# Twenty loads of the value cache, each issued as two transfers of 120 and 8 partitions

## The chip, the core and the metric

The kernel runs on one core of a Trainium2 chip. The core has five engines: TensorE (PE in the profile, with its weight loads as PEld), VectorE (DVE), ScalarE (ACT), GpSimd (POOL) and SyncE (SP). Data come from HBM (the tensors' home) into SBUF, a memory of 128 partitions, by DMA: 16 DMA engines work side by side, and a transfer is issued by an instruction of SP or ACT and tells of its landing on a semaphore. The metric is the device time of one execution in microseconds; the median of the runs is given.

## What is computed

A decode step of two alternating layer kinds, each applied twice to a residual stream x of 4 tokens (one per batch entry, width 448): attention over a cache, then a feed-forward layer. Only the last 2048 positions of the 8192 in the cache are used.

```python
def _A_ref(x, k_cache, v_cache, wq, wo):
    B, Sq, D = x.shape
    Hq, Dh = 16, 256
    Hkv, Sk = k_cache.shape[1], k_cache.shape[2]          # 8, 8192
    W = min(4096, max(256, Sk // 4))                      # 2048
    rep = Hq // Hkv
    q = (x @ wq).reshape(B, Sq, Hq, Dh).transpose(0, 2, 1, 3)
    k = jnp.repeat(k_cache[:, :, Sk - W:, :], rep, axis=1)
    v = jnp.repeat(v_cache[:, :, Sk - W:, :], rep, axis=1)
    p = _softmax(jnp.einsum("bhqd,bhkd->bhqk", q, k) * (Dh ** -0.5), axis=-1)
    o = jnp.einsum("bhqk,bhkd->bhqd", p, v)
    return o.transpose(0, 2, 1, 3).reshape(B, Sq, Hq * Dh) @ wo

def _B_ref(x, w_gate, w_up, w_down):
    return (_silu(x @ w_gate) * (x @ w_up)) @ w_down

x = x + _A_ref(_layernorm(x), A_k_cache, A_v_cache, A_wq, A_wo)
x = x + _B_ref(_layernorm(x), B_w_gate, B_w_up, B_w_down)
# ... and both once more, with the same caches and weights
```

All tensors are bf16. Both attention passes use the same keys and values.

## The kernel before, in words

**Units of work.** An attention pass over one token t (0 to 3) in layer l (0 or 1) and one key-value head kvh (0 to 7) is a *unit*, written as three digits "tlk". For a unit the kernel needs the keys (2048 x 256, 1 MB, two cells of SBUF) and the values (1 MB, loaded as two halves hv = 0 and 1 of 512 KB, one cell each). A cell is 4 KB in each of the 128 partitions; there are 31 cells and 7 more that are free once the q weights have been used for the last time. A value half is 1024 positions, eight of them in each partition: row q of a half is 4 KB that lie together in HBM, and goes to partition q.

**What happens to a unit.** DVE transposes the keys in place (`tr`, L887). PE forms the scores (`scores`, L920), the softmax goes over DVE, ACT and PE in small steps (L936 to L992), PE multiplies by the values (`pv`, L1001; its operand is the cell of the value half), then the result is turned (L1025), scaled (L1035) and sent through the output projection (L1047, L1055). When a token's eight heads are through, its residual, its norm, its feed-forward layer (L666 to L783) and the next q projection follow.

**Held data.** `HOLD` lists the keys and values that stay in their cells from layer 0 to layer 1. The others are loaded again for layer 1. In all SP issues 158 DMAs: 83 value halves (L897), 56 loads of keys (L875 for whole 1 MB ones, L881 for halves), 18 loads of x and weights (L521), one store.

**Order.** Nothing is planned at run time. `PLAN` gives the units' groups, `SEQ_PE`, `SEQ_DVE`, `SEQ_ACT`, `SEQ_POOL` and `SEQ_SP` the order of the instructions of each engine, by hand or by a search made before; `SLOTS` gives the cell of each load in SP's order. `Graph` finds which instruction must wait for which and places the waits (`_place_waits`). A load waits on SP until the last reader of its cell is through, and all loads behind it on SP wait with it. Each cell (or first cell of a pair) has a semaphore `h<cell>` of its own; a load adds 16 to it when it has landed (`_count`, `emit`), and its readers wait for the sum so far.

**Filler.** Entries `w1`, `w3` ... in `SEQ_PE` are matmuls of zeros into the accumulator A (L1137, and L543 when one follows another). They change no value.

**Places that matter here.** `Op` and `_count` (the amount that a load adds), `emit` (which issues it and attaches the semaphore), and in `group` the loop over `hv`, which makes one load per value half:

```python
g.dma(1 << 19, lambda e, cell=cell, hv=hv, vsrc=vsrc: e.dma_start(unit(cell), vsrc[hv]), None,
      w=(f"v{t}_{kvh}_{hv}",), cells=(cell,))
```

Of the kernel before, what the change touches and what calls it, by code (L numbers as in the profile page):

```python
# [34 lines left out]

ROWF = (1, 2)
PLAN = (
# [122 lines left out]

class Op:
    __slots__ = ("i", "eng", "kind", "emit", "deps", "nbytes", "dsem", "dval", "start", "end", "pos", "waits", "inc",
                 "val", "known", "cells", "rel", "bank", "tag", "run")

    def __init__(self, i, eng, kind, emit):
        self.i, self.eng, self.kind, self.emit = i, eng, kind, emit
        self.deps = {}
        self.nbytes = 0  # L170
        self.dsem = None
        self.dval = 0
        self.cells = self.rel = self.bank = ()
        self.inc = False
        self.val = 0
        self.waits = []


class Graph:
    tag = last_a = before = None  # L180
# [50 lines left out]

    def _count(self, o, sem):
        o.dsem = sem
        self.dcount[sem] = self.dcount.get(sem, 0) + 16
        o.dval = self.dcount[sem]

    def schedule(self, filler):
# [82 lines left out]
    def emit(self, eng_name, eng, sems, dsems):  # L320
        for o in self.order[eng_name]:
            for d in o.waits:
                if d.dsem is not None:
                    eng.wait_ge(dsems[d.dsem], d.dval)
                else:
                    eng.wait_ge(sems[d.eng], d.val)
            ins = o.emit(eng)
            if eng_name == PE:
                self.before = o.kind
            if o.dsem is not None:  # L330
                ins.then_inc(dsems[o.dsem], 16)
            elif o.inc:
                ins.then_inc(sems[eng_name], 1)
# [11 lines left out]
def build(nc, A_x, A_k_cache, A_v_cache, A_wq, A_wo, B_x, B_w_gate, B_w_up, B_w_down, out):  # L345
    s0 = A_k_cache.shape[2] - WIN
    g = Graph()

    with ExitStack() as es:
# [105 lines left out]
        for a in range(4):  # L455
            g.op(DVE, "d1", lambda e, a=a: e.memset(qmask[32 * a:32 * a + 32, a:a + 1], DH ** -0.5), r=("qmask",),
                 w=(f"qmask{a}",))
# [31 lines left out]
        for s_ in range(NS):  # L489
# [9 lines left out]
             w=("hmask",))  # L499
# [6 lines left out]
        for P in range(2):  # L506
# [5 lines left out]
             w=("lomask",))  # L512
# [334 lines left out]
        def unit(cell):  # L847
            return kv[:, HALF * cell[0]:HALF * cell[0] + HALF]

        def which(cell, kc):  # L850
            return int(cell[0] == max(kc[0][0], kc[1][0]))
# [7 lines left out]
        def group(gi, members, outs, split):  # L859
# [7 lines left out]
            for pp, t, layer, kvh in members:  # L867
                if layer == 1 and (t, kvh) in k_held:
                    kc, kk = k_held.pop((t, kvh))
                else:  # L870
                    kc, kk = [[], []], [f"k{pp}_{hf}" for hf in range(2)]
                    ksrc = A_k_cache[t, kvh, s0:s0 + WIN, :].rearrange("(p j) d -> p (j d)", p=128)
                    g.tag = ("k", t, layer, kvh)
                    if f"{t}{layer}{kvh}" in WHOLE.split():
                        g.dma(1 << 20, lambda e, kc=kc, ksrc=ksrc: e.dma_start(  # L875
                            kv[:, HALF * kc[0][0]:HALF * kc[0][0] + 2 * HALF], ksrc[:, :]), None, w=tuple(kk), cells=tuple(kc),
                            run=8192)
                    for hf, cell in enumerate(kc):
                        if f"{t}{layer}{kvh}" not in WHOLE.split():
                            g.tag = ("k", t, layer, kvh)  # L880
                            g.dma(1 << 19, lambda e, cell=cell, kc=kc, ksrc=ksrc: e.dma_start(  # L881
                                unit(cell), ksrc[:, HALF * which(cell, kc):HALF * which(cell, kc) + HALF]), None, w=(kk[hf],),
                                cells=(cell,))

                        def tr(e, cell=cell):
                            a = unit(cell).bitcast(UINT32).rearrange("p (k s) -> p k s", k=32)
                            return e.transpose(a, a)  # L887
                        g.tag = ("t", t, layer, kvh)
                        g.op(DVE, "tr", tr, w=(kk[hf],))
                vsrc = A_v_cache[t, kvh, s0:s0 + WIN, :].rearrange("(a q g) d -> a q (g d)", a=2, q=128)  # L890
                vs = [[], []]
                for hv, cell in enumerate(vs):
                    g.tag = ("v", t, layer, kvh, hv)
                    if layer == 1 and (t, kvh, hv) in v_held:
                        vs[hv] = v_held.pop((t, kvh, hv))
                    else:
                        g.dma(1 << 19, lambda e, cell=cell, hv=hv, vsrc=vsrc: e.dma_start(unit(cell), vsrc[hv]), None,  # L897
                              w=(f"v{t}_{kvh}_{hv}",), cells=(cell,))
                keep_k = layer == 0 and f"k{t}{kvh}" in HOLD.split()
                keep_v = [layer == 0 and f"v{t}{kvh}{hv}" in HOLD.split() for hv in range(2)]  # L900
                kcs.append(kc)
                kks.append(kk)
                vss.append(vs)
                free_k.append(not keep_k)
                free_v.append([not x for x in keep_v])
                if keep_k:
                    k_held[(t, kvh)] = (kc, kk)
                for hv in range(2):
                    if keep_v[hv]:
                        v_held[(t, kvh, hv)] = vs[hv]  # L910
# [3 lines left out]
            def scores(e, Ps):  # L914
                last = None
                for ce in range(8):
                    for x in range(X):
                        for P in Ps:
                            qd = 64 * P + 32 * x
                            last = e.matmul(Sb[s_][qd:qd + 8, 0:32 * 2 * J],  # L920
                                            lhsT=qe[q_][:, P, ce, :, :].rearrange("p a n -> p (a n)"),
                                            rhs=keys(kcs[P], J * x, J, ce), start=(ce == 0), stop=(ce == 7),
                                            skip_group_check=True)
                return last
# [5 lines left out]
            parts = [(P,) for P in range(n)] if split else [tuple(range(n))]  # L930
            for Ps in parts:
                kw = dict(acc=(f"s{s_}",)) if Ps[0] else dict(w=(f"s{s_}",))
                o = g.op(PE, "sch" if split else f"sc{n}" + "w" * (two - n + 1), lambda e, Ps=Ps: scores(e, Ps),
                         r=tuple(k for P in Ps for k in kks[P]) + tuple(f"qe{q_}_{P}" for P in Ps), bank=(f"S{s_}",), **kw)
# [61 lines left out]
            def pv(e, P, hv):  # L996
                last = None
                M = 4 if n == 1 else 8
                for a in range(2):
                    for gg in range(4):  # L1000
                        last = e.matmul(Yb[p_][32 * gg:32 * gg + M, 256:512],  # L1001
                                        lhsT=pT[pt][:, gg, 2 * a + hv, 4 * P:4 * P + M] if n == 2 else
                                        pf[:, 16 * gg + 8 * a + 4 * hv:16 * gg + 8 * a + 4 * hv + 4] if two else
                                        p1[:, gg % 2, 2 * a + gg // 2, hv, :, :].rearrange("p y n -> p (y n)"),
                                        rhs=unit(vss[P][hv])[:, 1024 * a + 256 * gg:1024 * a + 256 * gg + 256], start=False,
                                        stop=False, skip_group_check=True)
                return last
            for P, (pp, t, layer, kvh) in enumerate(members):
                for hv in range(2):
                    kw = dict(acc=(f"y{p_}",)) if hv or P else dict(w=(f"y{p_}",))  # L1010
                    o = g.op(PE, "pv", lambda e, P=P, hv=hv: pv(e, P, hv), r=(f"pT{pt}", f"v{t}_{kvh}_{hv}"),
                             bank=(f"Y{p_}",), **kw)
# [5 lines left out]
                 w=("oh",), bank=(f"Y{p_}",))  # L1018
# [49 lines left out]
        for si, (heads, splits) in enumerate(zip(plan(), plan_splits())):  # L1068
            where = {}
            for batch, split in zip(heads, splits):  # L1070
                members, outs = [], []
                for m in batch:
                    pos += 1
                    t, layer, kvh = m
                    done[(t, layer)] = done.get((t, layer), 0) + 1
                    if kvh not in where:
                        ts = sorted(t_ for b in heads for t_, _, k_ in b if k_ == kvh)
                        where[kvh] = (oc % 2, ts)
                        if used[oc % 2] != ts:
# [3 lines left out]
                                 w=tuple(f"oT{oc % 2}_{t_}" for t_ in range(B)))  # L1083
# [25 lines left out]
            for t, layer in full:  # L1109
                residual(t)  # L1110
                norm(t, xr)
                if layer == 0:
                    with_, waiting = waiting, []
                    if t in ROWF:
                        ffn_row(with_ + [t])
# [25 lines left out]
        dsems = {d: es.enter_context(nc.semaphore(f"d_{d}")) for d in g.dcount}  # L1141
# [60 lines left out]
```

## Time and profile before

| | |
|---|---|
| time, median of 3 runs | 277.35 us (276.79 to 277.89) |
| span of the profiled execution, first to last instruction | 277.7 us |
| HBM read | 100.77 MB, 363 GB/s over the span |
| DMA queue of the loads (q1) | 100.78 MB, 91.8% of 16 engines |
| instruction fetches (q8, q14) | 36 of 16 KB and 9 of 8 KB, 0.9% and 0.1% of 16 engines |
| PE, DVE, POOL, ACT busy | 242.4, 185.0, 80.4, 62.8 us |
| granted TensorE clock, mean | 0.984 |

No time of the profiled execution is given but its span; it lies within the three runs' times, and so stands for them.

How to read the rows. In a row of a window stand its bounds and length, then for PE, PEld, DVE, ACT and POOL the busy time with the number of instructions, then the granted clock, the mean busy share of the 16 DMA engines, and GB/s. A DMA share a little over 1 comes from packets whose records overlap by some nanoseconds. In a row of the chain in order of time stand start, length and what was worked on; "DMA half<-in_A_v_cache_dram" with a length is the time from the issue of a load to its landing, the time that it waited behind earlier loads included. A queue's row has packets, MB and the time of its packets as a share of 16 engines. In a row of issues the last number is the median time from issue to landing. In a row of a tile's instructions, a/b/c is the shortest, median and longest duration in ns.

### The profile page before, as it was taken

The page shows a single profiled execution, that of the slowest core. Times are in us where ns is not written, and L with a number is a line of the kernel's source. Part 1 is how long each engine was busy: PE and PEld are TensorE (multiplying, and loading weights), DVE is VectorE, ACT ScalarE, POOL GpSimd, SP SyncE. Part 2 cuts the span into 40 slices and gives each one's busy share as a digit, 9 for nine tenths or more (in the row PEclk, how much of TensorE's full clock was granted, in tenths as well). Part 3 has the DMA queues.
Part 4 walks back from the last instruction along what each step waited for, and adds up shares of the span by engine and source line. Part 5 has one row for each costly group of instructions (what it writes and reads, how often), then busy time and mean ns, then how long its engine had stood idle before and what let it go on. Part 6 is the DMA issues. An engine that isn't in the chain of part 4 may idle for free.

```text
span 277.7 us, 10576 instructions
## 1 busy us (share of the span) xinstructions
PE 242.4 (87%) x4751; PEld 126.5 (46%) x4576; DVE 185.0 (67%) x574; ACT 62.8 (23%) x173; POOL 80.4 (29%) x224
## 2 busy tenths in 40 slices
PE   3997999999999887998888887979799787989995
PEld 0121232233475553544445444535455456667664
DVE  4666817735612687978857599986768757389841
ACT  0003021111112222331332333224132321232411
POOL 1160121111024221615044243133234332254350
PEclk9998899999999999999999999999989999999998
DMA  7999999999999999999999999999999998799200
GB/s 278 425 420 413 415 395 418 399 401 406 405 387 417 411 412 414 410 409 411 351 394 400 414 417 411 408 413 408 358 384 350 411 378 297 279 396 411 81 2 3
DMA packets 25740, 101.44 MB, mean 365 GB/s; under 512 B 2523, under 2 KB 6623, under 8 KB 21471
## 3 DMA queue, kind: packets, MB, share of 16 engines
q1 hardware_dynamic: 25687, 100.78, 91.8%
q8 instruction: 36, 0.59, 0.9%
q14 instruction: 9, 0.07, 0.1%
q10 hardware_dynamic: 8, 0.00, 0.0%
HBM read 100.77 MB, written 0.00 MB: 363 GB/s over the span
## 4 chain that ended last, share of the span: by engine, by line
PE 40%; DMA 36%; DVE 14%; issue 3%; ACT 2%; SPq 2%; POOL 2%; DVEq 0%; ACTq 0%
DMA half<-in_A_v_cache_dram 24%; DMA half<-in_A_k_cache_dram 12%; DVE half L887 8%; PE S L920 8%; PE A L543 6%; PE Y L1001 6%; PE A L1137 5%; PE Z L740 3%; PE A L1055 2%; PE Z L776 2%; PE A L1047 1%; PE Y L969 1%; SPq L521 1%; DVE oh L1019 1%; SPq L897 1%
## 5 line engine op out<-in xcount | busy, mean ns | idle before, releaser
L887 DVE STREAM_TRANSPOSE half<-half 128x1024 uint32<-128x1024 uint32 x86 | 104.7, 1229 | 8.8 <-DMA half<-in_A_k_cache_dram 8.8
L1137 PE MATMUL A<-identb,small 128*128 128x512 bf16 x139 | 53.3, 389 | 3.3 <-DVE A L447 2.9
L1015 POOL TENSOR_TENSOR small<-small 128x2 f32<-128x2 f32 (+1 forms) x48 | 38.5, 805 | 47.1 <-DVE small L992 29.7
L543 PE MATMUL A<-identb,small 128*128 128x512 bf16 x175 | 51.8, 397 | 0.0
L920 PE MATMUL S<-half,qe 128*8 128x128 bf16 (+1 forms) x1520 | 45.0, 240 | 6.6 <-issue 2.8
L1001 PE MATMUL Y<-half,pT 128*8 128x256 bf16 (+1 forms) x1024 | 42.9, 274 | 8.4 <-DMA half<-in_A_v_cache_dram 5.0
L920 PEld LDWEIGHTS S<-half,qe 128*8 128x8 bf16 x1520 | 30.5, 84 | 22.3 <-DVE half L887 9.8
L954 ACT ACTIVATE praw<-S,small 104x128 bf16<-104x128 f32 (+2 forms) x48 | 19.4, 404 | 68.3 <-DVE small L950 64.1
L1019 DVE SCALAR_TENSOR_TENSOR oh<-oh,small,Y 128x256 bf16<-128x256 bf16 x48 | 22.5, 468 | 16.9 <-ACT oh L1017 16.7
L926 POOL TENSOR_TENSOR qe<-qc,tiny 128x64 bf16<-128x64 bf16 x64 | 18.1, 294 | 43.9 <-PE S L920 35.2
L1001 PEld LDWEIGHTS Y<-half,pT 128*8 128x8 bf16 (+1 forms) x1024 | 20.2, 84 | 23.0 <-DVE small L992 6.5
L1017 ACT ACTIVATE oh<-Y 128x256 bf16<-128x256 f32 x48 | 18.4, 383 | 45.8 <-PE Y L1001 37.3
L1137 PEld LDWEIGHTS A<-identb,small 128*128 128x128 bf16 x139 | 14.6, 105 | 14.9 <-issue 8.9
L577 POOL TENSOR_SCALAR st<-st 128x1 f32<-128x1 f32 x16 | 4.3, 267 | 57.6 <-DVE st L567 56.4
L978 ACT ACTIVATE pT<-Y 128x64 bf16<-128x64 f32 (+1 forms) x48 | 12.4, 258 | 36.0 <-PE Y L969 29.6
L1055 PE MATMUL A<-wo_sb,oT 128*4 128x448 bf16 x192 | 17.5, 356 | 2.0 <-issue 1.1
L1082 POOL MEMSET oT<- 128x16 bf16 x39 | 4.1, 112 | 38.4 <-PE A L1055 32.1
L992 DVE TENSOR_REDUCE small<-Y 128x2 f32<-128x32 f32 (+1 forms) x48 | 9.1, 189 | 8.8 <-PE Y L986 7.9
L1035 DVE TENSOR_TENSOR oT<-Y,small 128x4 bf16<-128x4 f32 (+1 forms) x63 | 9.0, 155 | 5.8 <-PE Y L1025 4.5
L950 DVE TENSOR_REDUCE small<-S 104x1 f32<-104x32 f32 (+1 forms) x48 | 8.5, 177 | 5.2 <-PE S L944 5.0
L941 PE MATMUL S<-small,identb 104*104 104x32 bf16 (+1 forms) x48 | 10.0, 208 | 1.9 <-DVE tiny L936 1.5
L1025 PEld LDWEIGHTS Y<-tiny,oh 128*128 128x128 bf16 x96 | 7.0, 98 | 9.6 <-DVE oh L1019 4.9
(139 smaller groups left out, 266.9 us busy)
## 6 DMA issues: line engine op xcount, KB each, us to landing
half<-in_A_v_cache_dram SPq DMA_DIRECT2D x83, 512.0 KB, 9.9
half<-in_A_k_cache_dram SPq DMA_DIRECT2D x30, 1024.0 KB, 11.2
half<-in_A_k_cache_dram SPq DMA_DIRECT2D x26, 512.0 KB, 8.9
wo_sb<-in_A_wo_dram SPq DMA_DIRECT2D x8, 448.0 KB, 17.2
half<-in_A_wq_dram SPq DMA_DIRECT2D x3, 1024.0 KB, 8.5
wd_sb<-in_B_w_down_dram SPq DMA_DIRECT2D x1, 1568.0 KB, 18.3
wg_sb<-in_B_w_gate_dram SPq DMA_DIRECT2D x1, 1344.0 KB, 18.0
wu_sb<-in_B_w_up_dram SPq DMA_DIRECT2D x1, 1344.0 KB, 20.8
```

The costliest lines, as they stand in the source:

```text
L543: return e.add_instruction(mybir.InstMatmult(start_tensor_calc=start, stop_tensor_calc=stop, ldweights=load, name=nc.get_next_instruction_ ...
L887: return e.transpose(a, a)
L920: last = e.matmul(Sb[s_][qd:qd + 8, 0:32 * 2 * J], lhsT=qe[q_][:, P, ce, :, :].rearrange("p a n -> p (a n)"), rhs=keys(kcs[P], J * x, J, c ...
L926: g.op(POOL, "qe", lambda e, P=P, t=t, kvh=kvh: e.tensor_tensor(qe[q_][:, P, :, :, :], qc[t][:, kvh, :, :].unsqueeze(2).broadcast_to([128, ...
L954: return e.activation(praw[0:R, 0:N].rearrange("p (g r l) -> p g r l", g=J, l=2), Sb[s_][0:R, 0:N].rearrange("p (l g r) -> p g r l", l=2, ...
L978: g.op(SCA, f"pt{n}", lambda e: e.activation(pf, Yb[p_][:, 0:PW], ACT.Copy), r=(f"yp{p_}",), w=(f"pT{pt}",), bank=(f"Y{p_}",))
L1001: last = e.matmul(Yb[p_][32 * gg:32 * gg + M, 256:512], lhsT=pT[pt][:, gg, 2 * a + hv, 4 * P:4 * P + M] if n == 2 else pf[:, 16 * gg + 8 * ...
L1015: g.op(POOL, f"pow{n}", lambda e: e.tensor_tensor(ri[p_][:, 0:2 * n], rs[p_][:, 0:2 * n], expo[:, 1:1 + 2 * n], op=ALU.pow), r=(f"rs{p_}", ...
L1017: g.op(SCA, "oh", lambda e: e.activation(oh[:, :], Yb[p_][:, 256:512], ACT.Copy), r=(f"y{p_}",), w=("oh",), bank=(f"Y{p_}",))
L1019: g.op(DVE, "oho", lambda e: e.scalar_tensor_tensor(out=oh[:, :], in0=oh[:, :], scalar=lomask[:, 0:1], in1=Yb[p_][:, 256:512], op0=ALU.mul ...
L1055: last = e.matmul(Ab[32 * k:32 * k + B, 0:D], lhsT=oT[oi][:, k % 2, k // 2, :], rhs=wo_sb[:, 4 * kvh + k, :], start=False, stop=False, ski ...
L1137: return e.matmul(Ab[:, 0:512], lhsT=w, rhs=rhs, start=False, stop=False, skip_group_check=True)
```

## The change

Twenty value halves, named by token, layer, head and half in `PARTED`, are loaded by two DMAs in place of one: the first for partitions 0 to 119, the second for partitions 120 to 127, issued one right after the other by SP. Each adds 16 to the cell's semaphore, so that the load as a whole adds 32, and every later count on that semaphore is higher by 16. Where the load stands in SP's order, which cell it fills, what it waits for, and who reads it stay as they are; so do the other 63 value halves.

```diff
+PARTED = "0011 0021 0060 0061 0071 1011 1070 1031 1041 2010 2061 2040 2071 3020 3000 3031 3040 2110 1111 3121"
...
     def _count(self, o, sem):
         o.dsem = sem
-        self.dcount[sem] = self.dcount.get(sem, 0) + 16
+        self.dcount[sem] = self.dcount.get(sem, 0) + 16 * o.parts
         o.dval = self.dcount[sem]
...
             ins = o.emit(eng)
+            if o.parts > 1:
+                for part in ins[:-1]:
+                    part.then_inc(dsems[o.dsem], 16)
+                ins = ins[-1]
...
-                        g.dma(1 << 19, lambda e, cell=cell, hv=hv, vsrc=vsrc: e.dma_start(unit(cell), vsrc[hv]), None,
-                              w=(f"v{t}_{kvh}_{hv}",), cells=(cell,))
+                        cut = (0, 120, 128) if f"{t}{layer}{kvh}{hv}" in PARTED.split() else (0, 128)
+
+                        def v_load(e, cell=cell, hv=hv, vsrc=vsrc, cut=cut):
+                            got = [e.dma_start(unit(cell)[a:b, :], vsrc[hv][a:b, :]) for a, b in zip(cut, cut[1:])]
+                            return got if len(got) > 1 else got[0]
+                        o = g.dma(1 << 19, v_load, None, w=(f"v{t}_{kvh}_{hv}",), cells=(cell,))
+                        o.parts = len(cut) - 1
```

More of the change, by code (lines that the diff above doesn't have):

```diff
@@ L164 @@
     __slots__ = ("i", "eng", "kind", "emit", "deps", "nbytes", "dsem", "dval", "start", "end", "pos", "waits", "inc",
-                 "val", "known", "cells", "rel", "bank", "tag", "run")
+                 "val", "known", "cells", "rel", "bank", "tag", "run", "parts")
     def __init__(self, i, eng, kind, emit):
@@ L176, in __init__ @@
         self.waits = []
+        self.parts = 1
 class Graph:
```

## The prediction

> **What bounds the kernel now.** I read the page from the top: engine shares, the slices of DMA, the DMA queues, the shares of the chain.
>
> ```profile
> span 277.7 us, 10576 instructions
> PE 242.4 (87%) x4751; PEld 126.5 (46%) x4576; DVE 185.0 (67%) x574; ACT 62.8 (23%) x173; POOL 80.4 (29%) x224
> ...
> DMA  7999999999999999999999999999999998799200
> ...
> q1 hardware_dynamic: 25687, 100.78, 91.8%
> q8 instruction: 36, 0.59, 0.9%
> q14 instruction: 9, 0.07, 0.1%
> ...
> PE 40%; DMA 36%; DVE 14%; issue 3%; ACT 2%; SPq 2%; POOL 2%; DVEq 0%; ACTq 0%
> ...
> L1137 PE MATMUL A<-identb,small 128*128 128x512 bf16 x139 | 53.3, 389 | 3.3 <-DVE A L447 2.9
> ...
> L543 PE MATMUL A<-identb,small 128*128 128x512 bf16 x175 | 51.8, 397 | 0.0
> ```
>
> PE looks busiest, but 53.3 + 51.8 = 105.1 us of its 242.4 are the filler matmuls, which give way. DMA is what runs without a break: nearly every slice from the first to the one at about 260 us is a 9 or an 8. The stretches say how full it is.
>
> ```profile
> 5.00:126.00 121.00, 111.58 (x1727) 45.44 (x1578) 73.54 (x219) 21.73 (x60) 28.16 (x73) 0.99 1.03 409
> 136.60:197.00 60.40, 51.53 (x1213) 30.34 (x1207) 46.36 (x135) 18.56 (x53) 20.94 (x59) 1.00 1.01 404
> 197.00:236.60 39.60, 33.25 (x747) 20.14 (x734) 29.43 (x82) 9.21 (x27) 12.10 (x35) 0.96 0.95 358
> 236.60:257.00 20.40, 19.57 (x467) 13.73 (x466) 14.89 (x53) 6.44 (x15) 8.53 (x23) 1.00 0.95 368
> ```
>
> The last two columns are the DMA share and GB/s: 1.03 and 409 over 121 us, 1.01 and 404 over 60 us. Only between 197 and 236.6 us does the queue run empty at places (358 GB/s). The chain in order of time agrees:
>
> ```profile
> 5.11 18.74 DMA half<-in_A_k_cache_dram
> ...
> 54.98 13.76 DMA half<-in_A_v_cache_dram
> ...
> 108.23 17.67 DMA half<-in_A_v_cache_dram
> ...
> 136.59 8.53 DMA half<-in_A_v_cache_dram
> ...
> 157.12 14.42 DMA half<-in_A_v_cache_dram
> ...
> 178.44 7.03 DMA half<-in_A_k_cache_dram
> ...
> 189.26 7.82 DMA half<-in_A_k_cache_dram
> 197.10 1.25 DVE half L887
> ...
> 246.35 12.98 DMA half<-in_A_v_cache_dram
> ```
>
> A transfer of 17.67 us is some 1.3 us of moving and the rest a place in the queue. So the landing at 125.9 us is the end of a stream that has run since 5 us, and work added to that stream anywhere ahead of it shows there. Likewise the landings at 145, 171, 185 and 197 us end a stream from 136.6, and the one at 259.3 a stream from 236.6. From 197 to 236.6 us the chain is work on the engines, and DMA waits for it.
>
> **Whose time it is inside a transfer.** A load is over when its last share is in, so the DMA engine that is furthest behind sets it. The last stretch shows the shares.
>
> ```profile
> DMA packets 2185, 8.01 MB, mean 334 GB/s; under 512 B 245, under 2 KB 245, under 8 KB 2180
> ...
> q1 hardware_dynamic: 2180, 7.93, 85.0%
> q8 instruction: 5, 0.08, 1.4%
> ...
> half<-in_A_v_cache_dram SPq DMA_DIRECT2D x8, 512.0 KB, 9.4
> half<-in_A_k_cache_dram SPq DMA_DIRECT2D x7, 512.0 KB, 8.5
> ```
>
> These are the queues from 236.6 to 260.6 us. Fifteen loads, (2180 - 245) / 15 = 129 packets each, that is one of 4 KB per partition, and 245 / 15 = 16 small ones, one end mark for each of 16 engines: eight rows per engine. Beside them five instruction fetches take 1.4% of 16 engines over 24 us, 5.4 us in all, 1.08 us apiece. Which engines they fall on shows in the tail, when no load is left to hide it:
>
> ```profile
> 257.00:257.25 0.25, 0.25 (x10) 0.20 (x6) 0.25 (x1) 0.25 (x2) 0.00 (x0) 1.00 1.01 393
> ...
> 257.75:258.00 0.25, 0.25 (x13) 0.23 (x11) 0.25 (x1) 0.04 (x1) 0.00 (x0) 1.00 0.45 180
> 258.00:258.25 0.25, 0.15 (x6) 0.06 (x3) 0.21 (x2) 0.19 (x1) 0.00 (x0) 1.00 0.32 131
> 258.25:258.50 0.25, 0.25 (x5) 0.17 (x5) 0.25 (x4) 0.00 (x0) 0.00 (x0) 1.00 0.28 115
> 258.50:258.75 0.25, 0.25 (x8) 0.09 (x4) 0.25 (x2) 0.00 (x0) 0.00 (x0) 1.00 0.28 115
> 258.75:259.00 0.25, 0.21 (x7) 0.00 (x0) 0.25 (x1) 0.00 (x0) 0.16 (x2) 1.00 0.16 66
> 259.00:259.25 0.25, 0.00 (x0) 0.00 (x0) 0.25 (x1) 0.24 (x1) 0.25 (x2) 1.00 0.24 98
> ```
>
> At 258.25 to 258.75 us 0.28 x 16 = 4.5 engines still run, after that 2.6 to 3.8. Had all five fetches gone to one engine, one (0.06) would be alone for some 5 us. They are spread: four or five engines are late by 1 to 2 us, the others are done. Over the kernel 36 fetches of 1.1 us (0.9% of 16 x 277.7 us is 40 us) are shared in the same way.
>
> **The change, part by part.** All 20 keys name loads that are issued. By the order in the code they are loads 5, 12, 21, 27, 35, 46, 58, 62, 69, 78, 86, 93, 99, 108, 115, 123, 129, 137, 143 and 154 of the SP queue's 158, one in about 13 us.
>
> *Bytes and waits*: the same 512 KB; one wait on the slot's semaphore for 32 more in place of 16. No instruction is added on PE, so 0.
>
> *SP issues*: twenty more.
>
> ```profile
> L897 SPq DMA_DIRECT2D half<-in_A_v_cache_dram x83: 327/433/12212, 2.4 to 246.8; - x83
> ```
>
> At the median of 0.433 us that is 8.7 us on SP. It lies under the backlog: a load lands 9.9 us after its issue at the median, and SP needs 0.43 us for what occupies DMA 1.28 us (512 KB at 409 GB/s). Behind the second issue wait SP's next loads. Where the queue is empty (load 143, at 236.70 us, the first after a gap) they come 0.43 us later, but the first part alone keeps DMA longer than that. I take 0; uncovered it is 0.43 us at three such places, 1.3 us.
>
> *Rows on the DMA engines*: this is the term that counts. 120 rows in shares of eight need fifteen engines, and the eight rows left need at least one and at most eight. The least that an engine serving both parts can get on top is one row of 4 KB: at 409 / 1.03 / 16 = 24.8 GB/s 0.165 us. The most is all eight rows on one engine, 8 x 0.165 = 1.3 us, a whole load's time once more. Below nothing it can go only if the engine that gets no row of the 120 is the last one each time (rival 2). I take one row, since a split over as many engines as there are rows is the nearest to how 128 rows are spread here, and because with four or five late engines at a time some of the late ones are likely among eight of 16.
>
> The sum: nine split loads come ahead of the landing at 125.9 us (load 72 is issued at 108.23), 9 x 0.165 = 1.49. Load 78 runs under engine work (126 to 136 us), 0. Loads 86, 93, 99, 108 and 115 lie in the stream from 136.6 to 197 us, 5 x 0.165 = 0.83. Loads 123, 129 and 137 fall where DMA waits for the engines, 0; with that cover gone 3 x 0.165 = 0.5. Loads 143 and 154 lie in the last stream, 0.33. Together 2.65 us.
>
> [...]
>
> **Rivals.**
>
> *1. No change.* The engines that get the extra row are not those that fetches make late. The tail has engines that finish 1 to 2 us before the last, against 0.33 us added there; if the eight are always among them, the split costs nothing: 277.35 us, within 1.4. Against it: eight of 16 would have to miss every late one.
>
> *2. Faster.* The engine that is left out of the 120 rows is the one that ends last at the landings that count. Then each such landing moves up to the next engine's end. In the tail the share falls to 0.16 at 258.75 and all data are in before 259.33, so the next engines end about 0.6 us earlier; for the three streams 3 x 0.6 = 1.8 us, 275.55. The most is full balance: the shares after 257.25 add up to an even end near 258.1, so 1.2 x 3 = 3.6 us, 273.75. It decides from the point where one engine alone is last; the share of 0.28 over half a microsecond speaks against it. [...]
>
> *3. Much slower.* A load of 120 rows or of eight isn't moved at the rate of 128. Every load in this trace has all 128 partitions, so no row shows another split. If two engines then get in each other's way at their destination, or the eight rows go one after another, a split load takes up to a second load's time: 1.3 us x 16 on the path = 20.8 us, 298.2; at half of that 10.4 us, 287.8. For it: the stream has no slack to hide it. Against it: nothing in the profile shows two engines disturbing each other. [...]
>
> **How the numbers follow.** The span of 277.7 lies inside the three times (276.79 to 277.89), so I add the sum to their median: 277.35 + 2.65 = 280.0 us. Chances: this forecast 0.37, rival 1 0.22, rival 2 0.15, rival 3 0.26. The forecast's own range, from a third of the sum to the sum with the uncovered terms (2.65 + 1.3 + 0.5), is 278.2 to 281.8. The whole range goes down to 275.7, most of rival 2's small gain, and up to 290, somewhat past half of rival 3. A change over 0.5% (1.4 us), about what a measurement of this kernel can tell from none, is likely upwards in the forecast and in rival 3 (0.61 together), downwards in most of rival 2 (0.14); the rest is 0.25.
>
> **What would show it.** Right: 20 more SP issues; a DMA share still about 1.0 to 126 us, but the landing of 125.9 about 1.5 us later, that of 197.1 about 2.3 later, and a tail of the same shape with four or five late engines. Rival 1: these landings stay. Rival 2: the tail ends nearer 258 us. Rival 3: GB/s in the stretch to 126 us falls well under 409 at a share still near 1.0, since packets take longer. Wrong altogether: if the stream from 5 us ends earlier by more than 0.6 us, fetches do sit on one engine. [...]

## The result, and the profile after

The changed kernel takes 322.38 us (median; 318.27 to 326.58), the kernel before, run beside it, 277.62 us. The ratio is 1.159, with an interval of 1.149 to 1.169: slower by 16%, some 44 us, or 2.2 us for each split load. The forecast was 280.0 us with a range up to 290.0. The direction was right, the size wrong by a factor of 17. Here and below, medians and ranges are of all runs of a kernel, while ratios and their intervals leave out runs over 1.5% above its fastest one.

The page of the changed kernel, the same parts as were shown of before:

```profile
span 319.9 us, 10596 instructions
...
PE 260.3 (81%) x4751; PEld 131.6 (41%) x4576; DVE 186.9 (58%) x574; ACT 62.6 (20%) x173; POOL 80.2 (25%) x224
...
DMA  7999999999999999999999999999999999799300
GB/s 295 345 420 325 405 311 367 328 291 405 391 295 412 415 300 291 387 321 346 299 359 317 281 403 264 379 287 367 344 326 351 285 372 283 250 402 326 133 3 3
DMA packets 25880, 101.44 MB, mean 317 GB/s; under 512 B 2663, under 2 KB 6763, under 8 KB 21611
...
q1 hardware_dynamic: 25827, 100.78, 92.4%
...
DMA 51%; PE 30%; SPq 9%; DVE 7%; issue 2%; ACT 1%; DVEq 0%
...
L1012 PE MATMUL Y<-half,pT 128*8 128x256 bf16 (+1 forms) x1024 | 50.0, 298 | 24.4 <-DMA half<-in_A_v_cache_dram 19.8
...
half<-in_A_v_cache_dram SPq DMA_DIRECT2D x63, 512.0 KB, 12.0
half<-in_A_k_cache_dram SPq DMA_DIRECT2D x30, 1024.0 KB, 15.0
```

The row of q1 says nearly all. The same 100.78 MB keep the 16 engines busy for 92.4% of a longer span: 0.924 x 319.9 = 295.6 us for an engine, where it was 0.918 x 277.7 = 254.9. So the engines spend 40.7 us more on the same bytes, out of 42.2 us by which the span grew. The slices of DMA are as full as before, and the GB/s in them, between the first one and the tail, swing between 250 and 420: the queue doesn't stand still, its packets take longer. The rest follows from late data. The multiplication by the values (L1001 before, L1012 now) waits 19.8 us for value loads where it waited 5.0, DMA has 51% of the chain where it had 36%, and a 1 MB load of keys, which nobody cut, lands 15.0 us after its issue in place of 11.2. The two rows of the page of before:

```profile
L1001 PE MATMUL Y<-half,pT 128*8 128x256 bf16 (+1 forms) x1024 | 42.9, 274 | 8.4 <-DMA half<-in_A_v_cache_dram 5.0
...
half<-in_A_k_cache_dram SPq DMA_DIRECT2D x30, 1024.0 KB, 11.2
```

One split load, seen close: the first one (load 5) moves between 10 and 13.5 us. These are stretches of the changed kernel, then one row for all of it up to 142 us, and behind them the stretch of 10 to 13.5 us in the kernel before (the last columns are DMA share and GB/s):

```profile
5.00:10.00 5.00, 4.27 (x14) 0.28 (x5) 3.40 (x18) 0.00 (x0) 0.00 (x0) 1.00 1.00 419
10.00:13.50 3.50, 3.31 (x15) 0.50 (x4) 1.10 (x15) 0.00 (x0) 0.26 (x1) 1.00 1.04 249
13.50:20.00 6.50, 5.67 (x38) 1.62 (x25) 4.58 (x25) 0.00 (x0) 3.98 (x12) 1.00 1.02 418
...
26.50:31.50 5.00, 3.67 (x30) 0.82 (x29) 3.74 (x10) 0.00 (x0) 0.79 (x3) 0.67 1.03 275
```

```profile
5.00:142.00 137.00, 115.79 (x1704) 44.61 (x1558) 71.37 (x213) 20.76 (x57) 28.06 (x73) 0.95 1.03 354
```

```profile
10.00:13.50 3.50, 3.25 (x19) 0.81 (x7) 1.81 (x22) 0.00 (x0) 0.53 (x2) 1.00 1.04 434
```

At a share of 1.04 in both kernels, 249 GB/s came through in place of 434: (434 - 249) / 434 x 3.5 = 1.5 us lost in one load. Before and behind the split load the rate is 419 and 418. The second one (load 12) lies between 26.5 and 31.5 us, at 275. The packet records say how: in the stretch from 10.4 to 12.2 us the 4 KB packets last 0.30 us at the median, where they last 0.159 in the kernel before. The 8 KB packets of load 6, which nobody cut and whose first ones move beside them, last 0.64 us in place of 0.309.

The tail is much as it was, a few late shares over 2 us. Each share's landing is an event of its own in the trace: the second split load has 23 of them, from 29.07 to 31.53 us, where a whole load has 16: as many as 15 shares and eight. For the load of keys right behind the first split load, and for the value half right behind the second, the 16 landings are (us, from the semaphore's records):

```
load 6   14.78 15.55 15.56 15.57 15.58 15.60 15.68 15.70 15.71 15.74 15.81 15.81 15.82 15.86 15.93 15.94
load 13  27.43 30.89 30.90 30.91 30.93 31.02 31.06 31.16 31.18 31.20 31.26 31.33 31.41 31.43 31.98 32.58
```

One engine is ahead, by 0.8 us after one split load and 3.5 us after two. The records don't number the engines; that it is the one without rows of the 120 is an inference: with 64 and 64 partitions (`e2_64_64` below) the first two landings of these loads lie 0.05 and 0.10 us apart. A load is over with its last share (in the kernel before, PE's L1001 waits for one whose 16 landings run from 66.88 to 68.74 us, and starts at 68.78), so this lead buys nothing.

### The profile page after: what moved, and what is told of

Read it like the earlier page. It is cut to its first block, busy times and chain, and to the rows that moved or that the text cites. A ratio compares the mean times of both kernels' runs of the same rounds, so it can differ in the third digit from the quotient of the medians.

```text
span 319.9 us, 10596 instructions
## 1 busy us (share of the span) xinstructions
PE 260.3 (81%) x4751; PEld 131.6 (41%) x4576; DVE 186.9 (58%) x574; ACT 62.6 (20%) x173; POOL 80.2 (25%) x224
## 3 DMA queue, kind: packets, MB, share of 16 engines
q1 hardware_dynamic: 25827, 100.78, 92.4%
## 4 chain that ended last, share of the span: by engine, by line
DMA 51%; PE 30%; SPq 9%; DVE 7%; issue 2%; ACT 1%; DVEq 0%
DMA half<-in_A_v_cache_dram 30%; DMA half<-in_A_k_cache_dram 16%; PE Y L1012 6%; SPq L906 6%; PE S L931 5%; DMA half<-in_A_wq_dram 5%; PE A L1148 4%; DVE half L893 4%; PE A L549 3%; PE Z L621 2%; SPq L527 2%; PE A L1066 2%; PE Z L746 1%; PE Y L980 1%; SPq L887 1%
## 5 line engine op out<-in xcount | busy, mean ns | idle before, releaser
L1012 PE MATMUL Y<-half,pT 128*8 128x256 bf16 (+1 forms) x1024 | 50.0, 298 | 24.4 <-DMA half<-in_A_v_cache_dram 19.8
L1148 PE MATMUL A<-identb,small 128*128 128x512 bf16 x139 | 56.1, 411 | 3.4 <-DVE A L453 2.9
L549 PE MATMUL A<-identb,small 128*128 128x512 bf16 x175 | 55.6, 421 | 0.0
L931 PE MATMUL S<-half,qe 128*8 128x128 bf16 (+1 forms) x1520 | 48.1, 251 | 7.4 <-DVE half L893 3.1
L931 PEld LDWEIGHTS S<-half,qe 128*8 128x8 bf16 x1520 | 32.4, 89 | 24.1 <-DVE half L893 11.5
L1012 PEld LDWEIGHTS Y<-half,pT 128*8 128x8 bf16 (+1 forms) x1024 | 21.3, 87 | 42.5 <-DMA half<-in_A_v_cache_dram 16.7
L1066 PE MATMUL A<-wo_sb,oT 128*4 128x448 bf16 x192 | 18.9, 386 | 4.5 <-DMA wo_sb<-in_A_wo_dram 2.7
L1003 DVE TENSOR_REDUCE small<-Y 128x2 f32<-128x32 f32 (+1 forms) x48 | 9.1, 190 | 11.2 <-PE Y L997 10.5
L961 DVE TENSOR_REDUCE small<-S 104x1 f32<-104x32 f32 (+1 forms) x48 | 8.6, 179 | 11.4 <-PE S L955 11.2
L952 PE MATMUL S<-small,identb 104*104 104x32 bf16 (+1 forms) x48 | 10.2, 213 | 4.5 <-DVE small L947 2.7
## 6 DMA issues: line engine op xcount, KB each, us to landing
wd_sb<-in_B_w_down_dram SPq DMA_DIRECT2D x1, 1568.0 KB, 19.8
```

The lines of the kernel that those rows point to most:

```text
L549: return e.add_instruction(mybir.InstMatmult(start_tensor_calc=start, stop_tensor_calc=stop, ldweights=load, name=nc.get_next_instruction_ ...
L931: last = e.matmul(Sb[s_][qd:qd + 8, 0:32 * 2 * J], lhsT=qe[q_][:, P, ce, :, :].rearrange("p a n -> p (a n)"), rhs=keys(kcs[P], J * x, J, c ...
L1012: last = e.matmul(Yb[p_][32 * gg:32 * gg + M, 256:512], lhsT=pT[pt][:, gg, 2 * a + hv, 4 * P:4 * P + M] if n == 2 else pf[:, 16 * gg + 8 * ...
L1066: last = e.matmul(Ab[32 * k:32 * k + B, 0:D], lhsT=oT[oi][:, k % 2, k // 2, :], rhs=wo_sb[:, 4 * kvh + k, :], start=False, stop=False, ski ...
L1148: return e.matmul(Ab[:, 0:512], lhsT=w, rhs=rhs, start=False, stop=False, skip_group_check=True)
```

## Experiments

Three theories stood after the result. **A**: a transfer to other than 128 partitions makes two DMA engines meet at one destination, and their packets take twice their time. **B**: a second DMA per load is dear by itself (issue, end marks, semaphore). **C**: the odd counts are at fault, 15 engines and eight, with unequal shares.

### The same loads cut along the row: `e1_columns`

```diff
-cut = (0, 120, 128) if ... else (0, 128)
+cut = (0, 1920, 2048) if ... else (0, 2048)
-e.dma_start(unit(cell)[a:b, :], vsrc[hv][a:b, :])
+e.dma_start(unit(cell)[:, a:b], vsrc[hv][:, a:b])
```

> The same 20 value halves in two DMAs each, but cut along the 4 KB of a partition (3840 B and 256 B), so both parts go to all 128 partitions. Theory A (two DMA engines meet at a destination whenever a transfer has other than 128 partitions, and then a 4 KB packet takes about 0.3 us in place of 0.16): no meeting here, so only 16 x 20 short packets more; 278 to 281 us. Theory B (a split load costs some 2.2 us by being two DMAs: a second issue on SP, a second set of end marks, a higher count): as slow as the changed kernel, about 322 us.

Measured: 279.01 us against 277.40, ratio 1.005 (1.000 to 1.009). From its page:

```profile
span 277.0 us, 10596 instructions
...
q1 hardware_dynamic: 28567, 100.78, 92.3%
```

Twenty more DMAs and 2880 more packets (28567 - 25687 = 20 x 144) cost some 1.3 us (0.0 to 2.5 by the interval), hardly more than can be told from nothing. B falls.

### 64 and 64 partitions: `e2_64_64`

```diff
-cut = (0, 120, 128) if ...
+cut = (0, 64, 128) if ...
```

> The same 20 halves cut into partitions 0 to 63 and 64 to 127; all 16 engines have equal shares, four rows of each part. [...] Theory C (only the odd count of 15 and 8 engines hurts: their shares are unequal, and the second DMA holds up SP): within 2 us of before, 276 to 280. Theory B: about 322.

Measured: 322.18 us, ratio 1.163 (1.154 to 1.172), as slow as the change. From its page, and the stretch of the first split load:

```profile
span 319.3 us, 10596 instructions
...
q1 hardware_dynamic: 26007, 100.78, 92.3%
```

```profile
10.00:13.50 3.50, 3.25 (x19) 0.81 (x7) 1.81 (x22) 0.00 (x0) 0.44 (x2) 1.00 1.04 291
```

The packets rise by 26007 - 25687 = 320, 16 end marks for each added DMA, as many as there are engines, and no engine is ahead behind the split loads (0.05 and 0.10 us, as said above). So C falls. The longer packets of A are there, at the size of A for the first load: (434 - 291) / 434 x 3.5 = 1.15 us lost, where an engine's eight packets at twice 0.159 us make 8 x 0.159 = 1.3. But twenty times that is 26 us, and the whole lost 45 us (0.163 x 277.4), 2.3 a load. Something adds to the doubled time.

### 112 and 16 partitions: `e3_112_16`

```diff
-cut = (0, 120, 128) if ...
+cut = (0, 112, 128) if ...
```

> The same 20 halves cut into 112 and 16 partitions: seven rows and one row on each of 16 engines, equal shares again, but neighbouring rows. [...] Theory C: within 2 us of before. Theory B: about 322.

Measured: 314.96 us, ratio 1.131 (1.121 to 1.141). That is 36 us lost, or 1.8 a load, though 112 and 16 rows divide evenly by 16 engines. The first split load, by the stretch:

```profile
10.00:13.50 3.50, 3.25 (x16) 0.61 (x6) 1.22 (x17) 0.00 (x0) 0.26 (x1) 1.00 1.05 337
```

It loses (434 - 337) / 434 x 3.5 = 0.78 us, little more than half of the 1.3 us that the doubled time of every packet makes. So on the mean its packets take less than twice their time.

### 32, 64 and 32 partitions: `e4_32_64_32`

```diff
-cut = (0, 120, 128) if ...
+cut = (0, 32, 96, 128) if ...
```

> The same 20 halves in three DMAs: partitions 0 to 31, 32 to 95 and 96 to 127. One issue more than any other kernel. [...] Theory B: twice the loss of the changed kernel, above 350. [...] Theory C: within 3 us of before.

Measured: 303.21 us, ratio 1.091 (1.084 to 1.099): 25.3 us. From its page and for its first split load:

```profile
span 302.2 us, 10616 instructions
...
q1 hardware_dynamic: 26327, 100.78, 92.4%
```

```profile
10.00:13.50 3.50, 3.25 (x18) 0.81 (x7) 1.49 (x20) 0.00 (x0) 0.26 (x1) 1.00 1.04 339
```

Three DMAs per load lose little more than half of what two lose (25.3 us against 45.2), and its first load loses (434 - 339) / 434 x 3.5 = 0.77 us. It is not the number of parts that counts: 303.21 us with three lies far from both B's "above 350" and C's "within 3 us of before". Nor do all rows of such a cut pay alike, for a doubled time of every packet would be the same 1.3 us a load in each of these cuts. The 4 KB packets agree: in the stretch from 10.4 to 12.2 us their median is 0.188 us, where `e2_64_64` has 0.284, and the fastest quarter is within 0.005 us of the usual 0.159.

The cuts side by side, by what the first split load lost and what all twenty lost on the mean:

| cut | first split load | mean of twenty |
|---|---|---|
| 120, 8 | 1.5 us | 2.2 us |
| 64, 64 | 1.15 us | 2.3 us |
| 112, 16 | 0.78 us | 1.8 us |
| 32, 64, 32 | 0.77 us | 1.3 us |

So of A this much is shown: when a load is cut across the partitions, packets take longer (at the median 0.30, 0.284 and 0.188 us in place of 0.159, for 120 and 8, 64 and 64, and 32, 64 and 32), and where it is cut sets how much is lost. Why is not shown. No record names an engine or a destination, and none tells which rows an engine gets. Nor do the runs tell the destination from the source: row q of a half is also its q-th 4 KB in HBM, so every cut across the partitions cuts the source in the same places. That engines meet at the destination stays a theory.

### Only the four loads held to be covered, and the other sixteen: `e5_off4`, `e6_on16`

```diff
-PARTED = "0011 0021 0060 0061 0071 1011 1070 1031 1041 2010 2061 ... 3031 3040 2110 1111 3121"
+PARTED = "2010 3031 3040 2110"                   # e5_off4
+PARTED = ...                                     # e6_on16: the other sixteen
```

> 120 and 8 partitions as in the change, but for loads 78, 123, 129 and 137 alone, those that the prediction held to be covered by work on the engines. If the cover holds: 277 to 279 us. If DMA has no slack there either: 4 x 2.2 = 9 us more, 286.

> The complement: the other 16 loads split into 120 and 8. If the four are covered while the others are split: as the changed kernel, about 322 us. If each split costs the same wherever it stands: 322 - 9 = 313.

Measured: ratio 1.039 (1.032 to 1.046), 288.45 us, for the four; 1.126 (1.115 to 1.136) for the sixteen. That is 10.8 us or 2.7 a load, and 35 us or 2.2 a load; together 46, the whole change within its interval. The four are not covered. From the page of `e5_off4`, and the stretch of its last three loads:

```profile
span 288.4 us, 10580 instructions
...
q1 hardware_dynamic: 25715, 100.78, 91.7%
```

```profile
208.00:247.00 39.00, 32.01 (x706) 19.01 (x694) 24.64 (x71) 8.22 (x25) 11.15 (x31) 0.91 0.99 326
```

Before, DMA was busy for 0.95 of 39.6 us between 197 and 236.6 us: 2 us of slack, enough for the 0.5 us that the prediction put there, not for three times 2. Now the share is 0.99, and DMA bounds that stretch as well. Load 78 had no cover at all, by a row of the kernel before:

```profile
126.00:136.00 10.00, 8.29 (x190) 4.58 (x190) 8.31 (x23) 2.22 (x6) 3.52 (x11) 1.00 1.00 398
```

Not all of the loss is packet time, though, in the run that was profiled (the slowest of the four, 290.18 us). Set against the kernel before, the landings in `e5_off4` come 3.1 us later behind load 78, and 6.8 us later at load 95, with nothing cut between them. In between, the granted clock (the column before the DMA share) was low from 138 to 150 us, and DMA was not full from 144 to 157 us:

```profile
138.00:144.00 6.00, 5.32 (x73) 2.82 (x72) 2.06 (x12) 0.86 (x3) 0.26 (x1) 0.56 0.99 386
144.00:150.00 6.00, 6.00 (x72) 2.41 (x71) 1.04 (x8) 2.19 (x5) 1.81 (x5) 0.59 0.79 283
150.00:157.00 7.00, 5.92 (x145) 3.89 (x146) 6.93 (x16) 1.22 (x4) 3.09 (x9) 1.00 0.81 259
```

In the kernel before the clock was 1.00 in all three stretches, and the DMA share was 1.01 and 1.03 in the last two. In `e5_off4` SP waited 4.7 us for PE's L1012 before it could issue load 86. So late data can also make later loads start late, by way of PE; why the clock was low there is not shown.

### What adds to the doubled time: `e7_early5`, `e8_late5`, `e9_early5_apart`, `e10_late5_apart`

All four cut five loads into 64 and 64, so that every engine has its share.

```diff
-PARTED = "0011 0021 ..."
+PARTED = "0020 0000 0051 0010 0050"              # e7_early5: loads 13 to 17
+PARTED = "2071 2070 2060 0111 0110"              # e8_late5: loads 99, 100, 101, 103, 104
+PARTED = "0011 0021 0060 0061 0071"              # e9_early5_apart: loads 5, 12, 21, 27, 35
+PARTED = "1031 1041 2061 2040 2071"              # e10_late5_apart: loads 62, 69, 86, 93, 99
```

> 64 and 64 partitions for five loads in a row near the start, loads 13 to 17, when one to three engines are late. If the loss per load is the doubled packet time alone: 5 x 1.3 = 6.5 us, 284. If it is 2.24 us for any split load (44.8 / 20): 11.2 us, 288.6. If being out of step is what adds to it, this one stays near 284 and the next kernel goes above 288.

> 64 and 64 partitions for five loads nearly in a row in the middle, loads 99, 100, 101, 103 and 104, when many engines are late by 1 to 3 us. Doubled packet time alone: 284. Out of step adds: 2.3 to 2.9 us a load, 289 to 292. If what adds is each passage between whole and split loads and not the lateness, both kernels of this pair pay it about once: 284 to 286 for both.

> 64 and 64 partitions for the five early loads of the change that stand apart from each other (5, 12, 21, 27, 35). The five early loads in a row cost 6.2 us. If only the doubled packet time counts: again 6.5 us, 284. If each passage from whole to split loads and back costs something too: 9 to 11 us, 287 to 289, since there are five such passages in place of one.

> The same for five loads of the middle that stand apart (62, 69, 86, 93, 99). The five in a row there cost about 9.5 us. If lateness of some engines alone adds to the doubled time: 9 to 10 us again, 287. If passages add as well: 12 to 14 us, 290 to 292; and more than the early five apart, if lateness adds too.

Measured, with the time that an engine of q1 is busy beyond the 254.9 us of before (share x span, from the pages below):

| five loads | ratio (interval) | us lost by it | q1 busy more, us |
|---|---|---|---|
| early, in a row | 1.020 (1.013 to 1.027) | 5.6 | 0.929 x 279.6 - 254.9 = 4.8 |
| middle, in a row | 1.037 (1.029 to 1.045) | 10.2 | 0.925 x 282.8 - 254.9 = 6.7 |
| early, apart | 1.032 (1.019 to 1.044) | 8.8 | 0.928 x 285.2 - 254.9 = 9.8 |
| middle, apart | 1.049 (1.041 to 1.057) | 13.6 | 0.919 x 291.7 - 254.9 = 13.2 |

```profile
span 279.6 us, 10581 instructions
...
q1 hardware_dynamic: 25767, 100.78, 92.9%
```

```profile
span 282.8 us, 10581 instructions
...
q1 hardware_dynamic: 25767, 100.78, 92.5%
```

```profile
span 285.2 us, 10581 instructions
...
q1 hardware_dynamic: 25767, 100.78, 92.8%
```

```profile
span 291.7 us, 10581 instructions
...
q1 hardware_dynamic: 25767, 100.78, 91.9%
```

Against what was expected: early in a row (284.2 us) is at the doubled time alone, early apart (288.2) in the range of the passages. Middle in a row (287.1) fell between the passages alone (284 to 286) and the lateness (289 to 292), and middle apart (292.6) just above the range in which both add up. By the times only the two groups in a row are told apart among neighbours (1.027 against 1.029 at the nearest); the other intervals overlap. The last column points the same way, with one profile behind each number; those of the two groups in a row come from the fastest of their four runs.

The landings tell more, load by load. For each load, take its last landing in a run less that of the same load in the kernel before. Each cut load adds a step to this difference. With them stands how many of the 16 shares of the load ahead landed over 0.3 us behind the median in the kernel before, that is, how many engines were late there:

| cut load, 64 and 64 | 5 | 12 | 21 | 27 | 35 |
|---|---|---|---|---|---|
| engines late in the kernel before | 0 | 1 | 2 | 3 | 4 |
| step in `e9_early5_apart`, us | 1.3 | 1.7 | 2.4 | 3.0 | 2.8 |
| of it on the uncut load right ahead, us | 0.4 | 1.6 | 1.7 | 2.3 | 2.0 |
| step in `e2_64_64`, us | 1.0 | 1.7 | 2.1 | 3.1 | 2.8 |

So standing apart is not dear by itself: load 5, cut while the engines were in step, costs the doubled time (1.3 us) and no more. The same cut costs up to 3.1 us where some are late, and most of that shows on the uncut load ahead of it. Loads 62 and 69 in `e10_late5_apart`, where the 16 landings of a load lie 3.3 us apart in the kernel before, cost 3.4 and 3.6 us. In a row it is paid once: in `e7_early5` the uncut load 12 is 1.7 us late, and the five cut loads behind it add only 4.0 us together.

A reading that would give this: at the passage from a whole to a split load, late engines are still on the load before and others already on the split one, and so get in each other's way. The packet records agree. 8 KB packets belong to whole loads alone (keys, q weights). The time of theirs above the usual 0.309 us, summed and divided by 16 engines, is 3.8 us before, 11.5 in the changed kernel, 3.7 and 4.2 with five in a row (early, middle), 4.8 and 7.1 with five apart. So loads that nobody cut do pay. Which engine crosses which was not seen, and no run changed the lateness at one place, so it is not shown that the lateness, and not something else about the place, sets the step. The size of the steps stays open.

## Why the prediction was right or wrong

*DMA bounds the kernel, a load is over with its last share, late engines are several*: right. One engine was 3.5 us ahead after two split loads, and that gained nothing, so rival 2 fell. The traces show several late engines and number none.

*Bytes, waits and SP issues at nothing*: right. `e1_columns` has the same twenty issues, waits and counts, and costs 1.3 us (0.0 to 2.5).

*Rows on the DMA engines, "I take one row"*: this is the step that failed. It reckoned what an engine has to move, and took each packet's time as given: 0.165 us of added work per split load. Measured are 40.7 / 20 = 2.0 us. In `e2_64_64`, with 16 end marks for each part and no engine ahead, the loss is the same. So the unequal shares, which the whole sum was made of, are not the cause. What costs is which partitions a part covers (`e1_columns`, with all 128 in both parts, costs nothing that can be told), and it costs through each packet's time, 0.30 us in place of 0.159.

*Its upper bound*: "a whole load's time once more", 1.3 us, was too low as well. With 64 and 64 it holds for a load cut while the engines are in step and for five in a row (1.0 to 1.3 us), but not for the loads cut where some engines are late (1.7 to 3.6 us). The prediction had no term for what a split load does to the uncut one ahead of it.

*The cover*: four loads were costed at nothing, and they cost 10.8 us. The rows had already said how thick the cover is: a share of 0.95 over 39.6 us is 2 us for three loads, and where load 78 moves, from 126 to 136 us, the share is 1.00. Part of the loss in the profiled run came another way, with a low granted clock and a DMA share of 0.79 and 0.81.

*Rival 3* had what the runs bear out: packets of a split load take nearly twice their time (0.30 us for 0.159). That two engines meet at the destination is its reading, which no run shows; nor is it shown why the four cuts lose different amounts in the first split load (1.5, 1.15, 0.78 and 0.77 us). It was given 0.26 and its middle, 287.8 us; what held it down was that "nothing in the profile shows two engines disturbing each other". But every load in that trace, save 3.5 KB of x in four partitions, had the one shape for which no run shows a loss, so its silence was no evidence. At full price the rival gave 298.2. Of the 24.2 us from there to 322.4, 10.8 are the four "covered" loads; the rest is what the other sixteen cost above 1.3 us each (2.2 by `e6_on16`).

*The range* ended a little past half of rival 3 and so left out the case in which its full price holds for every load.

*What would show it*: the signs named for rival 3 came (354 GB/s at a share of 1.03 up to 142 us, where it was 409). The queue has 25827 - 25687 = 140 packets more, seven for each split load: 23 end marks in place of 16.

## What to carry to other kernels

Where DMA bounds a kernel, look at which partitions a transfer covers before counting its bytes per engine: in this kernel a load cut along the row cost nothing that could be told, the same load cut across the partitions 1 to 2.7 us. A resource that every transfer of a trace uses in the same way shows no price for another way; then the dear end of the bounds needs its full weight. And a cover is as thick as the idle share of its stretch says, once for all that is put under it.

## What the runs showed of the hardware that was not expected

- Work for all 16 engines in every part is not enough: 64 and 64 partitions, with 16 end marks for each part, lose 45 us over twenty loads, and 32, 64 and 32 still 25 ((26327 - 25687) / 20 = 32 end marks more per load, 16 for each added DMA). 112 and 16 lose 36.
- Five early cut loads in a row keep the engines busy 4.8 us longer, five that stand apart 9.8 us. A cut load among whole ones costs 1.0 to 1.3 us while the engines are in step and up to 3.1 us where three or four of them were late, most of it on the uncut load ahead.
- In the changed kernel, whose data come late, PE's mean granted clock is 0.912 in place of 0.984, with PE busy for 81% of the span in place of 87% (L1012's matmul 298 ns, L1001's before 274). Beside 40.7 us of 42.2 on the DMA engines there is little room for it to have mattered for the time there; in `e5_off4` a clock of 0.56 to 0.59 went with 2.6 us of idle DMA.
